# Loads in pieces, early products of the identity, and weight chunks rounded one place sooner, at the start of an attention and feed-forward kernel

## The chip, the cores and the metric

The kernel runs on one core of one Trainium2 chip. The metric is the device time of one execution in microseconds, which is the time of that core. Engines are named as in the profile: PE is TensorE (PEld its weight loads), DVE is VectorE, ACT is ScalarE, POOL is GpSimd, SP is the engine whose queue issues the loads. All runs used for a comparison of times are of the state "fast".

## The reference

The input x (4 batches of 12416 rows of 128) goes through two attentions with 32 inducing points, then through a gated feed-forward block.

```python
def mab(q, kv):
    s = scale * (q @ kv.transpose(0, 2, 1))
    s = s - s.max(-1, keepdims=True)
    a = np.exp(s); a /= a.sum(-1, keepdims=True) + 1e-09
    return a @ kv
h = mab(I, x)                    # 32 rows per batch
y = mab(x, h)                    # 12416 rows per batch
xn = y / sqrt(mean(y * y) + 1e-06) * rms_g
out = (silu(xn @ w_gate) * (xn @ w_val)) @ w_out      # 128 -> 1536 -> 128
```

The three weights arrive as 64-bit floats and have to be rounded to 32 bits in the kernel. They are cut into nine chunks (i, c): i is 0 for w_gate, 1 for w_val, 2 for w_out, c is the third of the 1536 columns.

## The kernel before

Batch 0 is the start. Its x comes in seven sets (five of 16 rows per partition, one of 15, one of 2). TensorE turns each set into columns and makes scores; then come a maximum, exponentials, sums for h, and a chain that leads to the first products of the feed-forward loop.

```python
def load_rows(b, s):
    ...
    for t0, t1 in (((0, R), (R, 2 * R), (2 * R, n)) if not s else ((0, n),)):   # R is 4
        nc.sync.dma_start(out=t[:, t0:t1, :], in_=d[:, t0:t1, :])

def warm(n):                      # products that nobody reads
    ps = ps_acc.tile([P, 512], F32, name="acc")
    for _ in range(n):
        nc.tensor.matmul(ps[:, 0:P], ident[:], ident[:], start=True, stop=True)
```

Rounding a chunk is a sequence of small steps. VectorE masks out the exponent (power) and the upper mantissa bits (upper), ScalarE or VectorE makes numbers of them (power_number, upper_number), VectorE adds sign and lower bits (sign, lower), GpSimd multiplies the two parts, and the buffer of the raw words is filled with the next chunk.

```python
def sign():   # DVE
    nc.vector.scalar_tensor_tensor(out=e[:], in0=st["high"], scalar=-(1 << 31), in1=e[:], ...)
def lower():  # DVE, then POOL
    nc.vector.scalar_tensor_tensor(out=f[:], in0=st["low"].bitcast(U32), scalar=2.0 ** -52, in1=f[:], ...)
    nc.gpsimd.tensor_tensor(out=st["dst"], in0=f[:], in1=e.bitcast(F32)[:], op=ALU.mult)
    put()     # stores the chunk, and fetches the next raw one
```

The start, and the places of the chunks in the loop (k counts slots; a slot is one gate product, one value product and what hangs on them):

```python
for s in range(NS):
    for k in range(R):
        f["turn_x"](s, k)
    if s: f["scores1"](s - 1)
    if s == 2: parts(0, 0, nc.vector)       # power, power_number, upper, upper_number
    if s == 3: join(0, 0)                   # sign, lower
...
for s in range(NS):
    ...
    f["turn_e"](s)                          # DVE transposes e
    if s == 5: parts(1, 0)
    ...
    f["sum_h"](s)                           # PE
f["divide"](); f["turn_h"]()
...                                         # one chunk at each of the next few places
for k, one in ((0, (1, 1)), (3, (2, 1)), (7, (0, 2)), (10, (1, 2)), (13, (2, 2))):
    for j, name in ((0, "power"), (1, "power_number"), (1, "upper"), (2, "upper_number"), (2, "sign"), (3, "lower")):
        add(k + j, weight[one][name])
for k, *one in ((2, 0, 1), (5, 1, 1), (12, 0, 2), (15, 1, 2)):
    add(k, f["stack_of"], *one)             # PE product with the rounded chunk
    add(k, f["stack_low"], *one)            # DVE
```

Further names in the views: `stack_of` (L475) multiplies h with a rounded chunk of w_gate or w_val, L607 is the product with w_out, L657 and L662 are the gate and the value product, and `fold` adds up the four row groups of h before h is transposed (L409).

## Time and profile before

| | before |
|---|---|
| median of 3 runs | 1690.92 us (1689.47 to 1691.07) |
| TensorE busy | 98% of the profiled 1688.5 us |
| last scores of the first softmax end | 27.4 us |
| first gate product of the loop | 55.4 us |

The main views are shown in the prediction below. First, TensorE's timeline around 84 us: start, duration, engine and line, output from inputs, shape, count, and in brackets how long the engine was idle before it and what ended that.

```profile
83.97 0.39 PE L657 MATMUL gv<-a,sg 128*128 128x512 f32 x1
84.21 1.02 PE L607 MATMUL acc<-u,wo 128*128 128x512 f32 x2
84.66 0.80 PE L662 MATMUL gv<-a,sv 128*128 128x512 f32 x1
85.30 0.39 PE L657 MATMUL gv<-a,sg 128*128 128x512 f32 x1
86.93 1.13 PE L607 MATMUL acc<-u,wo 128*128 128x512 f32 x2 [1.24 <-POOL wo L283]
```

The sums for h on TensorE and the transposes of e that feed them on VectorE, from the timeline of the first 40 us.

```profile
31.73 5.63 PE L388 MATMUL gv<-xn,u 128*32 128x128 f32 x190
...
32.03 2.49 DVE L376 STREAM_TRANSPOSE u<-sc 128x512 f32<-128x512 f32 x4 [0.42 <-ACT sc L368]
```

TensorE does the 190 products without a hole, and four transposes run back to back beside them.

### The profile page before, as it was taken

To read this page: it belongs to the slowest core of one execution; us is meant where nothing else is said; L and a number is where in the kernel's file an instruction comes from. 1 tells how busy PE (TensorE), PEld (TensorE's weight loads), DVE (VectorE), ACT (ScalarE), POOL (GpSimd) and SP (SyncE) were. 2 spreads that over 40 slices of the span, in tenths; PEclk is the share of its full clock that TensorE was granted. 3 is DMA by queue.
4 is the path that set the end of the run, shared out by engine and by line. 5 is a ranking of instruction groups with operands and counts; after the bars stand their busy time and mean duration, and the time that the engine had idled before them with its cause. 6 is when DMAs were issued, how large, how long until landed. Compare 5 with 4: busy or idle time off the path is not lost.

```text
span 1688.5 us, 23205 instructions
## 1 busy us (share of the span) xinstructions
PE 1660.7 (98%) x6756; PEld 1036.6 (61%) x6756; DVE 1166.2 (69%) x1941; ACT 1237.4 (73%) x2216; POOL 1159.4 (69%) x931
## 2 busy tenths in 40 slices
PE   9989999999999999999999999999999999999998
PEld 6546665655676565665566666565557666666666
DVE  4877775676667776667667777676767666666665
ACT  4547777766787777776778777777677888788786
POOL 0336775777587775776668777577657888888884
PEclk9999999999999999999999999999999999999999
DMA  6445523433444131524335314252211111111111
GB/s 233 106 64 90 86 57 83 101 85 59 68 81 68 37 82 30 124 60 102 60 64 83 58 33 82 51 131 65 50 30 38 30 39 32 38 32 38 31 36 26
DMA packets 389454, 112.38 MB, mean 67 GB/s; under 512 B 365104, under 2 KB 369744, under 8 KB 386896
## 3 DMA queue, kind: packets, MB, share of 16 engines
q1 hardware_dynamic: 389136, 110.89, 32.1%
q8 instruction: 54, 0.88, 0.2%
q14 instruction: 72, 0.59, 0.1%
q10 hardware_dynamic: 192, 0.02, 0.0%
HBM read 53.95 MB, written 27.00 MB: 48 GB/s over the span
## 4 chain that ended last, share of the span: by engine, by line
PE 90%; ACT 2%; issue 1%; POOL 1%; DVE 1%; DVEq 0%; POOLq 0%; ACTq 0%
PE acc L607 42%; PE gv L657 17%; PE gv L662 16%; PE u L625 5%; PE u L623 5%; PE mm L330 3%; PE mm L509 1%; PE mm L388 1%; DVE u L664 1%; ACT silu L659 1%; ACT L659 1%; PE mm L461 0%; ACT L448 0%; POOL xn L650 0%; ACT sc L448 0%
## 5 line engine op out<-in xcount | busy, mean ns | idle before, releaser
L664 DVE TENSOR_TENSOR u<-silu,gv 128x512 f32<-128x512 f32 (+2 forms) x1200 | 788.0, 664 | 470.8 <-PE gv L662 236.0
L659 ACT ACTIVATE silu<-gv 128x512 f32<-128x512 f32 (+2 forms) x1200 | 698.6, 584 | 376.4 <-PE gv L657 340.0
L607 PE MATMUL acc<-u,wo 128*128 128x512 f32 (+2 forms) x1600 | 794.1, 580 | 3.5 <-DVE u L664 2.2
L662 PE MATMUL gv<-a,sv 128*128 128x512 f32 (+2 forms) x1188 | 760.2, 640 | 0.9 <-DVE u L664 0.6
L645 POOL TENSOR_TENSOR xn<-u,xn 128x512 fp32r<-128x512 f32 (+2 forms) x400 | 503.4, 1258 | 366.8 <-ACT xn L644 329.3
L650 POOL TENSOR_TENSOR xn<-hs,u 128x512 fp32r<-128x512 f32 (+2 forms) x400 | 503.6, 1259 | 39.3 <-ACT hs L649 36.1
L657 PE MATMUL gv<-a,sg 128*128 128x512 f32 (+2 forms) x1188 | 486.2, 409 | 6.0 <-ACT silu L659 6.0
L657 PEld LDWEIGHTS gv<-a,sg 128*128 128x128 f32 x1188 | 224.9, 189 | 238.3 <-ACT silu L659 120.6
L607 PEld LDWEIGHTS acc<-u,wo 128*128 128x128 f32 x1600 | 298.6, 189 | 82.6 <-issue 16.4
L662 PEld LDWEIGHTS gv<-a,sv 128*128 128x128 f32 x1188 | 224.7, 189 | 194.5 <-issue 137.7
L644 ACT ACTIVATE xn<-u 128x512 fp32r<-128x512 f32 (+2 forms) x400 | 247.7, 619 | 25.6 <-DVE u L664 23.7
L649 ACT ACTIVATE hs<-xn 128x512 f32<-128x512 f32 (+2 forms) x400 | 245.8, 614 | 4.9 <-POOL xn L650 4.0
L607 PE MATMUL acc<-xn,xn 128*128 128x512 f32 (+2 forms) x400 | 156.5, 391 | 4.5 <-POOL xn L650 4.5
L625 PE MATMUL u<-xn,xn 128*128 128x512 f32 (+2 forms) x400 | 155.7, 389 | 0.0
L623 PE MATMUL u<-xn,xn 128*128 128x512 f32 (+2 forms) x400 | 155.3, 388 | 0.0
L607 PEld LDWEIGHTS acc<-xn,xn 128*128 128x128 f32 x400 | 75.0, 188 | 24.2 <-POOL xn L650 7.6
L524 POOL TENSOR_TENSOR rs<-ms,mhalf 128x16 f32<-128x16 f32 (+2 forms) x28 | 75.9, 2709 | 16.9 <-DVE ms L522 15.1
L625 PEld LDWEIGHTS u<-xn,xn 128*128 128x128 f32 x400 | 75.2, 188 | 18.1
L623 PEld LDWEIGHTS u<-xn,xn 128*128 128x128 f32 x400 | 75.1, 188 | 16.8 <-issue 0.7
L616 DVE STREAM_TRANSPOSE o<-o 128x512 f32<-128x512 f32 (+2 forms) x97 | 67.7, 698 | 3.4
L615 DVE TENSOR_TENSOR o<-acc,o 128x512 f32<-128x512 f32 (+2 forms) x97 | 64.9, 669 | 0.0
L628 ACT ACTIVATE o<-u 128x512 f32<-128x512 f32 (+2 forms) x97 | 56.4, 582 | 0.0
(165 smaller groups left out, 745.1 us busy)
## 6 DMA issues: line engine op xcount, KB each, us to landing
out_dram<-o SPq DMA_DIRECT2D x320, 64.0 KB, 1.9
xn<-in_x_dram SPq DMA_DIRECT2D x62, 256.0 KB, 4.8
xT<-in_x_dram SPq DMA_DIRECT2D x60, 256.0 KB, 5.4
a<-hi SPq DMA_DIRECT2D x156, 64.0 KB, 2.0
a<-lo SPq DMA_DIRECT2D x156, 64.0 KB, 2.0
w<-w SPq DMA_DIRECT2D x22, 256.0 KB, 3.1
xn<-in_x_dram SPq DMA_DIRECT2D x4, 1024.0 KB, 10.9
out_dram<-o SPq DMA_DIRECT2D x64, 60.0 KB, 1.9
```

Of the source, the lines that this page charges most:

```text
L524: nc.gpsimd.tensor_tensor(out=rs, in0=ms, in1=mhalf[rows, 0:n], op=ALU.pow)
L607: nc.tensor.matmul(acc[:, 0:T], lhsT, rhs, start=st["left"] == NJ, stop=st["left"] == 1)
L623: nc.tensor.matmul(ups[:, 0:T], w[:, i, :], hi, start=st["k"] == nk, stop=False)
L625: nc.tensor.matmul(ups[:, 0:T], w[:, NK + i, :], lo, start=False, stop=not st["k"])
L644: nc.scalar.activation(hi, v, AF.Copy, scale=1.0 - 2.0 ** -13)
L645: nc.gpsimd.tensor_tensor(out=lo, in0=v, in1=hi.bitcast(F32), op=ALU.subtract)
L649: nc.scalar.activation(hs[:, 0:T], hi.bitcast(F32), AF.Copy, scale=1.0 + 2.0 ** -12)
L650: nc.gpsimd.tensor_tensor(out=d, in0=hs[:, 0:T], in1=v, op=ALU.subtract)
L657: nc.tensor.matmul(g[:, 0:T], sg[:, ts(j, P)], a[:, 0:T], start=True, stop=True)
L659: nc.scalar.activation(sl[:, 0:T], g[:, 0:T], AF.Silu)
L662: nc.tensor.matmul(v[:, 0:T], sv[:, ts(j, P)], a[:, 0:T], start=True, stop=True)
L664: nc.vector.tensor_tensor(out=t[:, 0:T], in0=sl[:, 0:T], in1=v[:, 0:T], op=ALU.mult)
```

## The change

The intent is that TensorE reaches its full clock sooner and that x reaches it in smaller pieces, and that rounded weight chunks are ready before TensorE asks for them. Chunk (1,0) is rounded within the first softmax, and each later chunk takes the place of the one before it.

```diff
-            for t0, t1 in (((0, R), (R, 2 * R), (2 * R, n)) if not s else ((0, n),)):
+            for t0, t1 in (((0, R), (R, 2 * R), (2 * R, n)) if not s else ((0, 2 * R), (2 * R, n)) if s in (1, full - 1) else ((0, n),)):
@@
-    warm(4)
+    warm(6)
@@ the raw gate chunk is fetched one set later
-        for _ in range(1 if s == 1 else 4 if s == NS - 1 else 0):
+        for _ in range(1 if s == 2 else 4 if s == NS - 1 else 0):
@@
             f["turn_x"](s, k)
+            if not s and k < 2:
+                warm(1)
-        if s == 2:
+        if s == 3:
             parts(0, 0, nc.vector)
-        if s == 3:
+        if s == 4:
             join(0, 0)
@@ chunk (1, 0), all on VectorE, between the steps of the maximum and of e
+    one = weight[1, 0]
     f["max1"]()
+    one["power"]()
     f["max2"]()
+    one["upper"]()
     f["max3"]()
+    one["power_number"](nc.vector)
@@ in the loop over sets, after turn_e(s)
-        if s == 5:
-            parts(1, 0)
+        if not s:
+            one["upper_number"](nc.vector)
+        if s == 1:
+            one["sign"]()
+        if s == 2:
+            one["lower"]()
+        if s == NS - 1:
+            parts(2, 0)
@@ (cut: (2,0), (0,1), (1,1) take the places of (1,0), (2,0), (0,1); the clamp of the power moves from power to power_number)
-            for k, one in ((0, (1, 1)), (3, (2, 1)), (7, (0, 2)), (10, (1, 2)), (13, (2, 2))):
+            add(0, weight[1, 1]["sign"])
+            add(1, weight[1, 1]["lower"])
+            for k, one in ((1, (2, 1)), (5, (0, 2)), (8, (1, 2)), (11, (2, 2))):
@@
-            for k, *one in ((2, 0, 1), (5, 1, 1), (12, 0, 2), (15, 1, 2)):
+            for k, *one in ((2, 0, 1), (4, 1, 1), (11, 0, 2), (13, 1, 2)):
```

More of the change, by code (lines that the diff above doesn't have):

```diff
@@ L238, in numbers, with power @@
                 engine.tensor_scalar(out=to[:], in0=t[:], scalar1=mul, scalar2=add, op0=ALU.mult, op1=ALU.add)
-        def power(engine=nc.scalar):
+        def power():
             if i < 2:
@@ L255, in power @@
                                     op0=ALU.logical_shift_right, op1=ALU.bitwise_and)
-            if engine is not nc.scalar:
-                nc.vector.tensor_scalar(out=e[:], in0=e[:], scalar1=896.0, scalar2=1151.0, op0=ALU.max, op1=ALU.min)
         def power_number(engine=nc.scalar):
             if wide:
+                e = st["e"]
+                if engine is not nc.scalar:
+                    nc.vector.tensor_scalar(out=e[:], in0=e[:], scalar1=896.0, scalar2=1151.0, op0=ALU.max, op1=ALU.min)
                 numbers("e", -896.0 * (1 << 23), float(1 << 23), engine)
@@ L683, in parts @@
         one = weight[i, c]
-        one["power"](*engine)
+        one["power"]()
         one["power_number"](*engine)
@@ L696 @@
             f["turn_x"](s, k)
+            if not s and k < 2:
+                warm(1)
         if s:
             f["scores1"](s - 1)
-        if s == 2:
+        if s == 3:
             parts(0, 0, nc.vector)
-        if s == 3:
+        if s == 4:
             join(0, 0)
     f["scores1"](NS - 1)
+    one = weight[1, 0]
     f["max1"]()
+    one["power"]()
     warm(4)
     f["max2"]()
+    one["upper"]()
     warm(3)
     f["max3"]()
+    one["power_number"](nc.vector)
     warm(8)
@@ L723 @@
     f["square_h"]()
-    weight[1, 0]["sign"]()
+    weight[2, 0]["sign"]()
     f["stack_of"](0, 0)
@@ L728 @@
     f["sub_max"](0)
-    weight[1, 0]["lower"]()
+    weight[2, 0]["lower"]()
     f["exp2"](0, 1)
@@ L735 @@
     square()
-    parts(2, 0)
+    parts(0, 1)
     f["stack_of"](1, 0)
@@ L740 @@
     scale()
-    weight[2, 0]["sign"]()
+    weight[0, 1]["sign"]()
     for i in range(2):
         f["stack_low"](i, 0)
-    parts(0, 1)
+    parts(1, 1)
     apply()
@@ L747 @@
     split()
-    weight[2, 0]["lower"]()
     spread(0, 0)
@@ L752 @@
     gather(0, 2)
-    join(0, 1)
+    weight[0, 1]["lower"]()
     flowing.append(True)
```

## The prediction

Its sum came to -3.8 us. A low window, here and below, is a stretch at half clock of 3.41 us, as long as the two in this trace (from 54.83 and from 126.51 us).

> **What bounds the kernel now.** I read the page's chain first, then the stretches of the first 130 us, then the timeline and the waits of TensorE inside them. All of the change lies before the eighteenth slot of the feed-forward loop (a slot is one gate product, one value product and what hangs on them), so the question is what TensorE loses in the first 90 us.
>
> The page, its busy line and its chain that ended last:
>
> ```profile
> PE 1660.7 (98%) x6756; PEld 1036.6 (61%) x6756; DVE 1166.2 (69%) x1941; ACT 1237.4 (73%) x2216; POOL 1159.4 (69%) x931
> ...
> PE 90%; ACT 2%; issue 1%; POOL 1%; DVE 1%; DVEq 0%; POOLq 0%; ACTq 0%
> ```
>
> TensorE is busy 98% of 1688.5 us. Whatever is gained must come from its idle time or from time in which it runs slowly, and most of both lies at the start. The timeline of the first 18 us, TensorE's transposes of x (L321), shows the slow part:
>
> ```profile
> 4.37 1.11 PE L321 MATMUL gv<-ident,xn 128*128 128x128 f32 x4
> ...
> 5.75 3.22 PE L321 MATMUL gv<-ident,xn 128*128 128x128 f32 x12 [0.27 <-DMA xn<-in_x_dram]
> ...
> 9.59 3.65 PE L321 MATMUL gv<-ident,xn 128*128 128x128 f32 x16 [0.62 <-ACT xT L324]
> ...
> 14.49 1.97 PE L321 MATMUL gv<-ident,xn 128*128 128x128 f32 x16
> ...
> 17.38 1.97 PE L321 MATMUL gv<-ident,xn 128*128 128x128 f32 x16
> ```
>
> Columns: start, duration, engine and line, output from inputs, count. Sixteen transposes of one set take 3.65 us at 9.59 and 1.97 us from 14.49 on: until about 13.9 us TensorE runs at half speed. From 14.49 on sets start every 2.89 us (14.49, 17.38, 20.27, 23.17) with TensorE full, while x lands every 2.5 us: set 1 was issued at 2.13 and took 7.3 us, so it landed at 9.46; set 2 landed at 13.2, set 3 at 15.7, set 4 at 18.2. So x is ahead of TensorE from set 2 on, and the slow start is passed on whole to the end of this part, 27.4 us.
>
> The stretches (columns: busy us of each engine, then clock, DMA share, GB/s) and TensorE's waits between 56 and 100 us:
>
> ```profile
> 54.90:58.20 3.30, 3.29 (x11) 2.28 (x10) 3.27 (x4) 1.62 (x3) 2.67 (x2) 0.50 0.68 203
> 126.60:129.80 3.20, 3.20 (x6) 1.67 (x5) 1.85 (x3) 0.63 (x2) 0.00 (x0) 0.50 0.27 68
> ...
> 57.00:87.50 30.50, 27.63 (x78) 13.81 (x76) 26.51 (x43) 18.46 (x32) 8.07 (x7) 0.98 0.50 113
> ```
> ```profile
> PE acc L607 <- POOL wo L283: 1.2, 1, 1.2
> PE mm L475 <- POOL hs L283: 0.7, 1, 0.7
> PE mm L475 <- POOL w L283: 0.6, 2, 0.4
> PE gv L662 <- DVE sv L480: 0.3, 1, 0.3
> ```
>
> In the loop's first 30.5 us TensorE is idle 2.87 us, all of it for weights that are not rounded yet: L283 is the last step of rounding a chunk. VectorE is full there too (26.51 of 30.5). Twice the clock falls to 0.50 for 3.4 us, each time after a TensorE wait (1.69 us before L563 at 53.57; 2.7 us before L607 at 125.03).
>
> [...]a transpose every 0.213 us at first, then every 0.109; the low stretches last 3.41 us. [...]9.59 to 13.9 holds nearly nothing but transposes and ended in full speed. [...]the trace shows 431 to 439 GB/s between 9.6 and 16.4 us[...]. [...]here one masking step (L254) takes 0.42 us alone and 1.14 beside a GpSimd multiply.
>
> **The change, part by part.**
>
> *(a) Load and clock.* Set 1 comes as two halves (the first should land near 8.2 instead of all at 9.46), the gate chunk goes behind set 2, set 5 is cut too. warm(6) for warm(4) adds 4 products (each warm is two passes of 0.213 us), filling 3.2 to 4.05 while x is awaited; two single ones fill 5.3 to 5.75 and 6.65 to 7.05. So TensorE is busy from 1.35 to about 8 us without a hole over 0.1. The full clock began at 13.87 by the trace[...]: full clock by about 7 to 8.2. Set 1 is then done at 10.4 (bound by its second half), scores of set 0 take 1.0, set 2 has landed at about 12.0, set 3 at 15.7 as before, since the same bytes lie ahead of it. Set 3's transposes start at 15.78 and not at 17.38; after it TensorE binds as before. **-1.6 us**. DMA now sets this start, so a still faster clock gives no more.
>
> *(b) Chunk (1,0) moves into the softmax.* Six VectorE steps (0.42, 0.42, 0.43, 0.43, 0.69, 0.69 by the same steps of chunk (0,0) and (1,0)) go between the maximum and the transposes of e. The first four fit in holes: VectorE waited 0.45 before L345, 0.47 before L354, 0.88 and 0.42 before the transposes. Perhaps +0.1. The last two stand between the second, third and fourth transpose, which ran back to back (four in 2.49). TensorE takes 0.93 for each set of sums, transposes come every 0.62; with 0.62 more ahead of the third, then of the fourth, TensorE waits 0.3 twice: **+0.65**. In return (2,0)'s first steps move to where (1,0)'s were, all later chunks move up one place, and one chunk's 0.84 us of masking and one 0.69 leave the loop.
>
> *(c) Stage 38 to 55 us.* The same steps at the same places with another chunk. After the split only one 0.69 step is left before the first L664, where before there were three (the last one 1.77 long): the first u came at 57.07 although its silu was done at 56.83: **-0.2**.
>
> *(d) The loop's first slots.* Slots are about 1.33 us of TensorE. (1,1): its last step is at slot 1, its product at slot 4, before 3 and 5: the 0.7 goes. (0,2): 8 and 11 for 10 and 12: the 0.35 goes. (1,2): 11 and 13 for 13 and 15, the same distance, so its 0.26 stays, but the value product of slot 16 no longer waits for it: 0.31 goes. (2,2): last step at 14 and not 16: the 1.24 goes. Sum 2.6; as VectorE remains nearly full I take **-2.5**. The fetches behind them come earlier too, as each waits for the chunk before.
>
> *(e) Clock windows.* The two low windows cost an estimated 0.7 (around the loop's start, where latency hides part) and 1.7 us (half of 3.4). [...]Mean **-0.25**, but a swing of about 1.5.
>
> Sum: -1.6 + 0.1 + 0.65 - 0.2 - 2.5 - 0.25 = -3.8, so 1687.1 us.
>
> **Rivals.** *VectorE takes over in slots 0 to 14.* u, four and a half chunks of about 2.2 to 2.6 us and four stack steps come to some 22 us for 15 slots, 1.47 a slot against TensorE's 1.33. The trace's 26.51 of 30.5 speaks for it; against it, eight u buffers let VectorE lag, and the work is 1.5 less than before. It would leave half of (d): 1688.4. *The clock does not rise sooner*[...]: (a) still gets something, as set 1's first half fills the hole before 9.59, but only about 0.8: 1688. *The holes were already hidden* behind the 2.7 us wait at 125 or the exponentials at 107: [...]both move with the loop, so I doubt it; it would be 1690. *No cost in (b)*, if TensorE has slack at the sums: 1686.4.
>
> **Range and chances.** Nothing in the steady part changes, so 2% (34 us) is out of reach either way. The three runs before span 1.6 us; with (d) uncertain by 1.3 and (e) by 1.5, I take 1684.7 to 1689.4. Faster by over 2%: 0.005; within: 0.99; slower: 0.005.
>
> **What would show it.** (a) transposes of sets 1 to 3 at 1.97 us for sixteen, the last scores at about 25.8 and not 27.4. (b) two waits of TensorE of about 0.3 us for the transposes of e. (c) the first gate product at about 54.6. (d) TensorE's waits for L283 in the loop under 0.6 in sum. (e) where the clock is 0.50. Wrong if the early clock comes late, if the loop keeps 2 us of waits, or if a low window appears or goes: then only the clock view tells the parts apart.

## More of the kernel before

The product with wo (L607) normally starts 0.24 us after a gate product (83.97, 84.21). At 86.93 it starts 1.63 us after one, because chunk (2,2) was not rounded yet.

## The result, and the profile after

The changed kernel takes 1684.78 us (median of 4 runs, 1683.21 to 1685.48) against 1690.6 us for the kernel before (4 runs, 1689.47 to 1691.07). The ratio is 0.9965 with a 95% interval of 0.9948 to 0.9983. A ratio here is the mean time of one kernel's fast runs over that of the other's of the same rounds, so it is not quite the ratio of the medians. The mean of the four runs is 1684.56 us, 5.9 less than before. The prediction had 1687.1, 3.8 less, and a range of 1684.7 to 1689.4.

The page's busy line, the stretches and TensorE's waits between 55 and 100 us, in the changed kernel. The columns of the stretches are the busy times of PE, PEld, DVE, ACT and POOL, then clock, DMA share and GB/s.

```profile
PE 1657.2 (98%) x6764; PEld 1034.8 (61%) x6764; DVE 1165.0 (69%) x1944; ACT 1235.8 (73%) x2214; POOL 1159.1 (69%) x931
```
```profile
119.40:122.70 3.30, 3.30 (x6) 1.99 (x7) 2.59 (x5) 0.70 (x2) 1.28 (x1) 0.50 0.16 40
...
57.00:87.50 30.50, 30.50 (x100) 15.59 (x98) 27.30 (x50) 17.06 (x30) 7.46 (x6) 1.00 0.51 104
```
```profile
PE acc L608 <- DVE u L665: 0.3, 1, 0.3
```

In the loop's first 30.5 us TensorE was busy 27.63 us in 78 products and is now busy all 30.50 us in 100. Every wait for a weight is gone. VectorE is a little fuller than it was (27.30 us for 26.51). One stretch at half clock is left, at 119.4.

The start, on TensorE (lines are one higher than before, L322 for L321):

```profile
7.07 1.10 PE L322 MATMUL gv<-ident,xn 128*128 128x128 f32 x8
8.97 1.07 PE L322 MATMUL gv<-ident,xn 128*128 128x128 f32 x8 [0.81 <-ACT xT L325]
10.23 1.06 PE L322 MATMUL gv<-ident,xn 128*128 128x128 f32 x8 [0.19 <-ACT xT L325]
11.22 1.06 PE L331 MATMUL gv<-xT,indT 128*32 128x512 f32 x8
12.71 1.94 PE L322 MATMUL gv<-ident,xn 128*128 128x128 f32 x16 [0.42 <-DMA xn<-in_x_dram]
```

The transposes are at full speed from about 7 us on (one every 0.109 us, after one every 0.213), and TensorE now waits for x. The wait before 8.97 stands under ScalarE, but that set's first half landed at 8.84, as its load was issued at 2.13 and took 6.7 us. The sums for h, on the same engine:

```profile
30.79 6.28 PE L389 MATMUL gv<-xn,u 128*32 128x128 f32 x190
```

They take 6.28 us where they took 5.63. The record shows only two holes in them, of 0.11 and 0.12 us, at 33.05 and 34.25.

The start times of TensorE's landmarks show where the time came from. Gate products are counted from 0. From the last scores to gate product 38 a stretch repeats to 0.05 us in all runs that leave it alone, so there a single profile settles most questions. Three stretches do not repeat so well. The start hangs on when x lands: the last scores end at 26.22 to 27.57 us (mean 26.86) in the seven traces with the changed start, and at 27.44 and 27.89 in the two with the old one. Gate product 38 to 50 hangs on the clock (see below), and gate product 50 to the end differs by 0.3 us among kernels that are the same there.

| stretch | before | changed | difference |
|---|---|---|---|
| start to the end of the last scores | 27.44 | 26.50 | -0.94 |
| last scores to first sum for h | 4.29 | 4.29 | 0 |
| first sum for h to the transpose of h (L409) | 6.74 | 7.39 | +0.65 |
| transpose of h to the first product of the loop's input (L563) | 15.10 | 14.68 | -0.42 |
| that product to gate product 2 | 3.70 | 3.00 | -0.70 |
| gate product 2 to gate product 20 | 33.37 | 29.17 | -4.20 |
| gate product 20 to 50 | 50.03 | 49.94 | -0.09 |
| gate product 50 to the end | 1547.81 | 1548.07 | +0.26 |
| sum | 1688.48 | 1683.04 | -5.44 |

### The profile page after: what moved, and what is told of

Read it like the earlier page. It is cut to its first block, busy times and chain, and to the rows that moved or that the text cites. A ratio compares the mean times of both kernels' runs of the same rounds, so it can differ in the third digit from the quotient of the medians.

```text
span 1683.0 us, 23231 instructions
## 1 busy us (share of the span) xinstructions
PE 1657.2 (98%) x6764; PEld 1034.8 (61%) x6764; DVE 1165.0 (69%) x1944; ACT 1235.8 (73%) x2214; POOL 1159.1 (69%) x931
## 4 chain that ended last, share of the span: by engine, by line
PE 93%; ACT 2%; DVE 1%; issue 1%; DMA 1%; POOL 1%; SPq 0%; DVEq 0%; POOLq 0%; ACTq 0%
PE acc L608 43%; PE gv L658 17%; PE gv L663 16%; PE u L626 5%; PE u L624 5%; PE mm L331 3%; PE mm L510 1%; PE mm L389 1%; DMA xn<-in_x_dram 1%; ACT silu L660 1%; DVE u L665 1%; ACT L660 1%; POOL rs L525 0%; PE gv L322 0%; PE mm L462 0%
## 5 line engine op out<-in xcount | busy, mean ns | idle before, releaser
L608 PE MATMUL acc<-u,wo 128*128 128x512 f32 (+2 forms) x1600 | 793.5, 580 | 2.6 <-DVE u L665 2.5
L608 PEld LDWEIGHTS acc<-u,wo 128*128 128x128 f32 x1600 | 298.3, 189 | 81.1 <-issue 16.6
L608 PE MATMUL acc<-xn,xn 128*128 128x512 f32 (+2 forms) x400 | 156.7, 392 | 4.5 <-POOL xn L651 4.5
L608 PEld LDWEIGHTS acc<-xn,xn 128*128 128x128 f32 x400 | 75.1, 188 | 24.3 <-POOL xn L651 7.7
```

Of the source, the lines that this page charges most:

```text
L608: nc.tensor.matmul(acc[:, 0:T], lhsT, rhs, start=st["left"] == NJ, stop=st["left"] == 1)
```

## The experiments

The theory after the first look was this. The loop gained nearly twice what I had taken, because a wait costs TensorE more than the hole that the trace shows before it (4.20 us gained for 2.87 us of holes); the start gained less, because cutting a set makes x land later (set 3 at 16.33 for 15.71). The rivals were that the loop's gain belongs to the low clock window that was there before and is not there now, or to one chunk's work less on VectorE.

### The extra products alone

```diff
 (kernel before)
-    warm(4)
+    warm(6)
             f["turn_x"](s, k)
+            if not s and k < 2:
+                warm(1)
```

> The kernel before with the extra products of the identity alone (warm(6), and one product after each of set 0's first two groups); loads, chunks and loop as before. Theory E (the early full clock is what part 1 of the change gains): full clock by 7 to 8.2 us, set 3's transposes start near 15.8 us and not 17.38, the last scores end near 25.8 and not 27.44, and the time falls by about 1.6 us, more than the 0.94 that the whole change got there. Rival (the clock stays low because set 1 in one piece leaves a hole before 9.5 us): set 3 still at 17.4, time within 0.3 us of before. The loop's first slots (gate product 2 to gate product 20) stay at 33.4 us under both.

Measured: 1689.78 us (1689.66 to 1691.85), ratio to before 0.9999 (0.9984 to 1.0014). The trace has the full clock from 4.22 us, set 3 at 16.67 and the last scores at 26.73, 0.71 less than before. Set 3 landed at 16.15 and TensorE, full from 13.80 on, was behind it. Neither expectation holds: the clock came early even though there was a hole of 1.50 us before set 1 at 10.05, and the gain is less than half of 1.6. In the time it does not show beside the spread of the runs.

This run settled another point. It has no low window at the loop's start, and the stretch from L563 to gate product 2 takes 3.00 us like the changed kernel's, but gate product 2 to 20 takes 34.05 (33.4 was expected). Together that is 37.05, and 37.07 in the kernel before, which had the low window. TensorE's waits between 55 and 100 us in this run:

```profile
PE acc L607 <- POOL wo L283: 1.2, 1, 1.2
PE acc L607 <- DVE u L664: 0.8, 1, 0.8
PE mm L475 <- POOL hs L283: 0.7, 1, 0.7
PE mm L475 <- POOL w L283: 0.6, 2, 0.3
PE gv L662 <- DVE sv L480: 0.3, 1, 0.3
```

The 0.70 us that the low window cost at the loop's start was given back before gate product 20: without it, TensorE only waits longer, 0.8 us before an L607 that had no such wait in the kernel before. So the loop's gain from the chunks has to be read from L563 on, and is 37.05 - 32.17 = 4.9 us.

### The cut and the later gate chunk alone

The edits to load_rows, to the fetch of the gate chunk and to the places of chunk (0,0), on the kernel before.

> The kernel before with the two-piece loads of sets 1 and 5 and the gate chunk behind set 2 alone; no extra products. If the extra products are needed for the early clock: full clock at 13.9 us as before or one window (3.41 us) sooner at best, set 3 at 16.5 to 17.0, gain 0.4 to 0.9 us. If the cut itself makes the loads late (set 3 landed at 16.33 in the changed kernel, 15.71 before), set 3's landing shows 16.3 here too; if that was chance of one execution, 15.7.

Measured: 1689.94 us (1689.29 to 1691.54), ratio 0.9999 (0.9984 to 1.0014). The full clock began at 11.30, set 3 landed at 16.86 and started at 17.00, the last scores ended at 27.03, 0.41 less than before. So with the cut alone the full clock began 2.57 us sooner than in the kernel before (13.87), in one execution of each, and set 3 lands late here too.

### The changed kernel with sets 1 and 5 in one piece

```diff
-... else ((0, 2 * R), (2 * R, n)) if s in (1, full - 1) else ((0, n),)):
+... else ((0, n),)):
```

> The changed kernel with sets 1 and 5 loaded in one piece again (extra products, the gate chunk behind set 2, and chunks as changed). If the cut costs the 0.62 us by which set 3 landed later: set 3 lands at 15.7 and its transposes start near 15.8, last scores near 25.9 (changed kernel 26.50), time 0.6 us below the changed kernel. If the late landing was chance, or came from the order and not the cut: no difference over 0.2 us in the last scores. If the hole left by the one-piece set 1 holds the clock down: set 3 at 17 and 0.6 us or more above the changed kernel.

Measured: 1684.37 us (1682.67 to 1684.71), ratio to before 0.9962 (0.9946 to 0.9979), not to be told from the changed kernel. Set 3 landed at 16.06, but the last scores ended at 27.37: the third case that I had written, in the trace; the 0.6 us that it gave for the time did not show. Set 1 came at 9.94 after a hole of 1.49 us, and the clock, full from 6.83, fell back:

```profile
10.30:13.60 3.30, 3.30 (x19) 2.81 (x21) 0.00 (x0) 2.00 (x4) 0.00 (x0) 0.50 1.03 429
```

In the first run above nearly the same hole (1.50 us) was not followed by half clock. Why the one was and the other not is not shown. The first rise to full clock comes at 4.22 to 14.35 us in the fourteen traces.

### The chunks alone

The changed kernel with loads, gate chunk and products as before.

> The changed kernel with loads, gate chunk and products of the identity as before: only the places of the weight chunks are changed. Theory L (the waits for unrounded weights cost more than the idle time that the trace shows before them, 4.2 us for 2.87 us): gate product 2 to gate product 20 takes 29.2 us as in the changed kernel (33.4 before), whatever the start does; last scores at 27.4; the sums for h end 0.65 us later against their start than before; time 1686.3 to 1686.9 if the clock windows fall as before. Rival (part of the 4.2 us was the loop starting earlier against the loads, or the low clock window): 30.5 us or more for the same stretch.

Measured: 1684.91 us (1682.96 to 1687.63), ratio 0.9969 (0.9954 to 0.9984). Gate product 2 to 20 takes 29.15 us, the sums cost 0.65 more, the last scores ended at 27.89. **The chunks alone give nearly the whole change**: 5.4 us by the medians of this round, where the changed kernel had 5.8 by the medians of its own. The median is 1.4 us below the band that I expected. The four runs spread over 4.7 us, more than I expected, and the trace says why. The clock was at half for 6.83 us near 120, in the slowest of the four runs:

```profile
120.20:126.90 6.70, 6.11 (x10) 3.48 (x11) 3.93 (x7) 1.81 (x3) 1.82 (x2) 0.50 0.37 73
```

Gate product 38 to 50 measures it. It takes 17.5 us in the traces without a low window there, 18.9 to 19.2 with one window and 20.5 with two. Over the eleven traces that have the 2.7 us hole before it, none appeared three times, one six times, two twice.

### The old places in the loop

```diff
-for k, one in ((1, (2, 1)), (5, (0, 2)), (8, (1, 2)), (11, (2, 2))):
+for k, one in ((3, (2, 1)), (7, (0, 2)), (10, (1, 2)), (13, (2, 2))):
-for k, *one in ((2, 0, 1), (4, 1, 1), (11, 0, 2), (13, 1, 2)):
+for k, *one in ((2, 0, 1), (4, 1, 1), (12, 0, 2), (15, 1, 2)):
```

> The changed kernel with the four chunks that are still rounded inside the loop at the places of before ((2,1) at 3, (0,2) at 7, (1,2) at 10, (2,2) at 13, their products at 12 and 15); chunk (1,0) stays in the softmax and (1,1) early. Theory P (the places decide[...]): the holes before the second chunk's products and before the product that needs (2,2) come back, 0.3, 0.3, 0.3 and 1.2 us, and gate product 2 to gate product 20 takes 31.8 to 32.3 us (29.2 in the changed kernel, 33.4 before). Rival (one chunk fewer on VectorE inside the loop is what freed TensorE): 29.2 to 30.0 us, holes under 0.6 in sum.

The expected band allows about 0.2 us for each wait beyond its hole, an estimate from the 4.2 us gained for 2.87 us of holes.

Measured (one run, 1687.11 us, state unknown, so only the stretches are used): gate product 2 to 20 takes 32.40 us (0.1 over the expected band), 3.23 more than in the changed kernel. The waits came back:

```profile
PE acc L608 <- POOL wo L284: 1.2, 1, 1.2
PE mm L476 <- POOL w L284: 0.6, 2, 0.4
PE acc L608 <- DVE u L665: 0.3, 1, 0.3
PE gv L663 <- DVE sv L481: 0.3, 1, 0.3
```

VectorE had the same number of steps in the loop as in the changed kernel, so the rival "one chunk fewer on VectorE" falls: the places decide. The four holes that are new are 1.24, 0.35, 0.27 and 0.31 us, 2.17 in sum, and cost 3.23. That is 0.27 us for each wait on top of its hole.

### One wait by itself

```diff
-... (11, (2, 2))):
+... (13, (2, 2))):
```

> The changed kernel with chunk (2,2) alone rounded from slot 13 instead of 11, so that its last step is at slot 16 as before. If a wait costs the idle time that the trace shows: one hole h before the product with wo near slot 18, and gate product 17 to 20 grows by h over 5.17 us. If the idle time is read short, because the record of the product before reaches past the moment at which the next could have started: it grows by h + 0.2 to 0.3 us. h is between 0.6 and 1.3.

Measured (one run, 1687.50 us, state unknown): gate product 17 to 20 takes 6.67 us, 1.50 more than in the changed kernel (5.17), and this is the only stretch of the loop that grew. The hole is 1.23:

```profile
80.91 0.41 PE L658 MATMUL gv<-a,sg 128*128 128x512 f32 x1
81.15 1.02 PE L608 MATMUL acc<-u,wo 128*128 128x512 f32 x2
81.61 0.80 PE L663 MATMUL gv<-a,sv 128*128 128x512 f32 x1
82.24 0.40 PE L658 MATMUL gv<-a,sg 128*128 128x512 f32 x1
83.87 1.13 PE L608 MATMUL acc<-u,wo 128*128 128x512 f32 x2 [1.23 <-POOL wo L284]
84.43 0.80 PE L663 MATMUL gv<-a,sv 128*128 128x512 f32 x1
```

From gate product to L608 it is 0.24 us when nothing waits (80.91, 81.15) and 1.63 here, 1.39 lost. From L608 to the value product it is 0.46 (81.15, 81.61) and 0.56 here, another 0.10. The sum is 1.49. **The hole of 1.23 is what is left of 1.39 after the 0.16 us by which the record of the gate product reaches past the moment when the next product could have started.** The expectation was right on this.

### Chunk (1,0)'s last steps later

```diff
-        if s == 1:
+        if s == 3:
             one["sign"]()
-        if s == 2:
+        if s == 5:
             one["lower"]()
```

> The changed kernel with the last two VectorE steps of chunk (1,0) one after the fourth and one after the sixth transpose of e, where TensorE has slack. If those two steps cost the start 0.65 us: from the first sum for h to the product of fold takes 5.56 us as in the kernel before (6.21 in the changed one), no hole over 0.05 there, and 0.65 us less in all unless the clock windows move. Rival (something else, such as GpSimd's multiply, delays the transposes): still 6.1 or more.

Measured: 1685.53 us (1685.09 to 1686.51), ratio 0.9969 (0.9954 to 0.9984), no gain in time. The first sum to fold takes 5.57 as expected, so these two steps are what the sums waited for. But to the transpose of h it takes 7.07 (7.39 in the changed kernel): half was lost again. VectorE's timeline says where:

```profile
35.78 0.39 DVE L254 TENSOR_SCALAR we<-sc 128x512 int32<-128x512 int32 x1
36.09 1.50 DVE L267 TENSOR_SCALAR o<-sc 128x512 int32<-128x512 int32 x1
37.51 0.15 DVE L401 RECIPROCAL rl<-gv 128x1 f32<-128x1 f32 x1
```

Chunk (2,0)'s masking L267 took 1.50 us, where it takes 0.42 alone, beside GpSimd's multiply for (1,0), which the move had brought to the same moment. The reciprocal came late.

### That masking after the division

```diff
 (the edit above, and)
-            parts(2, 0)
+            weight[2, 0]["power"]()
+            weight[2, 0]["power_number"]()
     f["divide"]()
+    weight[2, 0]["upper"]()
+    weight[2, 0]["upper_number"]()
     f["turn_h"]()
```

> The changed kernel with the last two steps of chunk (1,0) after the fourth and sixth transpose of e, and chunk (2,0)'s second masking after the division. The run with the first of these moves ended the sums 0.64 us sooner and lost it again before the division, where VectorE was late. Theory (VectorE's work before the division is the bound of this stretch, not the places alone): first sum for h to the transpose of h takes 6.75 to 7.0 us (7.39 in the changed kernel, 7.07 with the first move, 6.74 before). Rival: 7.0 or more, the masking is missed later and the time comes back by the first gate product.

Measured: 1683.61 us (1682.59 to 1686.03), ratio 0.9961 (0.9947 to 0.9974). The first sum to the transpose of h takes 6.74 us, as in the kernel before, and nothing comes back later. The 0.65 us are avoidable. They came from the places of the two steps, and what was lost again in the run before came from the collision: VectorE stands idle for 0.93 us before the reciprocal here, which would have held the masking at its 0.42 us alone, but not at 1.50. No run separates this from my theory that the amount of VectorE's work is the bound, so for that part it is worked out and not shown.

```profile
36.98 0.17 DVE L401 RECIPROCAL rl<-gv 128x1 f32<-128x1 f32 x1 [0.93 <-PE gv L399]
```

### One piece, with the hole filled

The changed kernel with sets 1 and 5 in one piece, and warm(5) after set 0's last group.

> The changed kernel with sets 1 and 5 in one piece and five more products of the identity after set 0, which fill TensorE's hole of 1.5 us before set 1. If cutting set 1 costs landing time (set 3 landed 8.7 to 8.9 us after set 0's last piece in the four uncut runs, 8.9 to 9.5 in the six cut ones) and the hole costs the clock: full clock by about 7 to 8.5 us in every execution, set 3's transposes start at 16.1 to 16.3 (16.47 to 17.53 in the cut runs), the last scores end at 26.0 to 26.4. If not: 26.5 or later.

Measured: 1683.34 us (1682.94 to 1684.44), ratio 0.9958 (0.9944 to 0.9972). The full clock held from 6.16 us, set 3 landed at 16.18 and started at 16.32 (0.02 past the expected band), the last scores ended at 26.35. Set 3 landed at 15.71 to 16.18 in the six uncut traces (mean 16.06) and at 16.05 to 17.40 in the eight cut ones (mean 16.71). The cut costs about 0.65 us of landing on average, with a wide spread. The delay is there when the last piece of set 1 lands (9.80 to 11.16 us in the cut traces, 9.46 to 9.92 in the uncut ones); after it each MB takes 2.5 us in both. Why the two halves take longer than the whole I did not find out. In the time the uncut version with the filled hole is not to be told from the changed kernel.

### Without the split product before the second hole

The 2.7 us hole near 120 is in both kernels. GpSimd's power and a multiply stand before a step of a product that is split into three.

```diff
-            if (j not in KJ or b == 0 and u < 2 or ...
+            if (j not in KJ or b == 0 and u < 3 or ...
```

> The changed kernel, where the product of unit 2, j = 9 is no longer split into three on GpSimd, so that GpSimd's power (2.9 us) and its multiply do not stand before a step that TensorE waits for. Theory: the 2.7 us hole before L608 near 119.4 us goes, with it the low clock window of 3.41 or 6.83 us that follows it in most executions, while one plain product costs 0.2 us more than the split one; time 2.5 to 4.5 us below the changed kernel, spread of the runs smaller. Rival (the next split product takes over the same wait): a hole of 1 us or more before another L608 near 122, gain under 1.5.

Measured: 1683.61 us (1682.51 to 1684.67), ratio 0.9957 (0.994 to 0.9973). The gain of 2.5 or more did not come. A hole of 2.40 us is still there, now before another L608, and VectorE stands before it:

```profile
119.12 0.71 DVE L533 STREAM_TRANSPOSE aT<-sc 128x512 f32<-128x512 f32 x1 [2.30 <-POOL sc L529]
119.75 0.65 DVE L665 TENSOR_TENSOR u<-silu,gv 128x512 f32<-128x512 f32 x1
```

On VectorE the next u stands behind that transpose, which waited 2.3 us for the same GpSimd chain, so u was late. My rival had named the wrong successor, but it was right that the wait would move. The spread of the runs (2.2 us) did not shrink to that of the next section.

### And that transpose later

```diff
 (the edit above, and)
-(32, 33, 33, 34, 34, 36, 38)
+(32, 33, 33, 34, 34, 38, 40)     # the gathers that follow go two slots later too
```

> The run without the split product of unit 2, j = 9, and in addition the transposes of the second set's weights (L533) two slots later (38 for 36), with its split and its gathers two slots later too. That run still had a hole of 2.4 us, because VectorE itself stood 2.3 us before L533 for GpSimd's multiply. Theory: with both moved neither TensorE nor VectorE waits for that chain; gate product 20 to 38 as there, 38 to 50 takes 14.8 to 15.2 us (17.27 there, 19.13 in the changed kernel), no low clock window near 120 in any execution, time 1681.0 to 1682.0, spread under 1 us. Rival (the hole moves on to the gathers or to a split product): 38 to 50 stays over 16.5.

Measured: 1681.26 us (1681.24 to 1681.36), ratio 0.9945 (0.993 to 0.996). Gate product 38 to 50 takes 15.27 us (19.13 in the changed kernel; a little over the expected band). There was no low window, and the four runs lie within 0.12 us. The later transpose without the other edit was not run. TensorE's waits between 110 and 124 us:

```profile
PE acc L608 <- POOL xn L651: 0.7, 1, 0.7
PE u L626 <- POOL xn L646: 0.3, 1, 0.3
```

### All of these together

The edits of the last four sections and the uncut sets with the filled hole, together.

> The changed kernel with the three edits together (later seam and no split product of unit 2, j = 9; the softmax's rounding steps later; sets 1 and 5 uncut with five more products). If they are independent: 1680.0 to 1681.2 us, the changed kernel's 1684.8 less 3 to 4 for the seam and less 0.4 to 0.8 for the start. If the start's gain is taken back at the first gate product by GpSimd's power: 1681.2 to 1682.

Measured: 1680.59 us (5 runs, 1680.46 to 1680.97), ratio to before 0.9941 (0.9929 to 0.9954). It is the fastest version and gives the right result. Its stretches are those of the parts: last scores at 26.34, sums to transpose 6.74, gate product 38 to 50 15.28. The parts are independent.

## Why the prediction was right or wrong

*What bounds the kernel* was right: all that changed by more than 0.3 us lies before gate product 20, and TensorE's waits for unrounded weights were the largest part.

*Step (d), "Sum 2.6; as VectorE remains nearly full I take -2.5", failed in its size.* With (c)'s -0.2 it stood for 2.7 us from L563 to gate product 20; the chunks gave 4.9. The mechanism was the one named: the holes went. I took each wait for the hole in the trace. The runs with the old places and with (2,2) alone show that a wait costs its hole and 0.27 us more. The five holes of the run with the extra products alone are 0.71, 0.34, 0.27, 0.32 and 1.24, 2.88 in sum, and with five times 0.27 they are worth 4.2. Another 0.5 is the wait for the first u, which shrank from 0.84 to 0.31; in the kernel before it was hidden by the low window. These make 4.8 of 4.9. The rest I did not resolve. I had also counted 0.26 of (1,2) as staying; it went, although the distance of its two places was kept. And I had lowered the sum for a full VectorE. That rival fell: VectorE was busy 27.30 of 30.5 us, and TensorE waited for it only before the first u (0.31 us). Its sum was even too low: 15 steps and 4 steps of 0.69 us with 4.5 chunks of 2.2 to 2.6 make 23 to 25 us and not 22.

*Step (a), -1.6, was too large.* The early clock came, at 4.35 to 7.25 us in the seven traces with the changed start (about 7 to 8.2 was expected). The failing term is "Set 3's transposes start at 15.78", which took the landing of set 3 as fixed "since the same bytes lie ahead of it". It landed at 16.33, and at 16.71 on average over the cut runs. The profiled gain was 0.94, in one execution; by the seven traces with the changed start against the two with the old one it is 0.8. In the time neither the extra products nor the cut alone gave anything that shows (a ratio of 0.9999 for both).

*Step (b), +0.1 and +0.65, was right*: 0 and 0.65. Its mechanism was confirmed by moving the two steps. The sign that it named, two waits of about 0.3 us, came as two holes of 0.11 and 0.12: these too cost more than they show. It counts six VectorE steps where there are seven; the clamp of 0.42 us is missing, and it cost nothing here.

*Step (c)* had -0.2 for the first u. The transpose of h to L563 also shortened by 0.42: the product z on VectorE starts 1.23 us after the products with gram (L510) instead of 1.65. It does so in all eleven traces with the changed chunks and in none of the other three. The product behind those, which waits for GpSimd's rounded chunk, does not explain it: it starts 0.96 us after them in both kernels, and GpSimd's multiply ends 0.49 us after their start in both. The cause stays open.

*Step (e)* was wrong in one half. The low window at the loop's start costs nothing by gate product 20, as the loop waited for weights anyway, and it was in no trace but that of the kernel before. The other costs 1.3 to 1.7 us, or 2.9 when it lasts two windows, near the 1.7 estimated; it came in 8 of the 11 traces that have the 2.7 us hole before it. It appears in both kernels. That it is most of the spread of their runs is likely and not shown for each: the granted clock of an execution goes with its time (0.999 in the two faster runs of the chunks alone, 0.998 and 0.997 in the two slower).

The predicted 1687.1 was thus too high by 2.3 us against the median and 2.5 against the mean; 0.5 of the latter is the kernel before, taken as 1690.9 where the four runs have a mean of 1690.4. In the profiled pair the difference was 5.4 us for the predicted 3.8: (d) with (c) gained 2.2 more than predicted, the transpose of h to L563 another 0.4, and (b) cost 0.1 less; against that (a) gained 0.7 less, and (e) 0.4 less (a gain of 0.25 was expected, and 0.17 was lost after gate product 20).

## What to carry to other kernels

When an engine waits in a stream of instructions whose records overlap, measure the wait by the distance of starts, with it and without it, and not by the hole before the instruction; here holes of 0.3 us cost nearly twice that. Look for the wait that takes over when one is removed: two engines waited for the same GpSimd chain here, and moving one away left the other. And a hole in TensorE can cost more than itself through the clock. Here holes of 1.49 us (sets 1 and 5 in one piece) and 1.69 us (before L563 in the kernel before) were each followed by a stretch at half clock (0.50 over 3.3 us), and the hole of 2.7 us by 3.41 or 6.83 us of it in 8 of 11 traces, which cost 1.3 to 2.9 us; holes of 1.50 us (extra products alone) and 1.26 us (before L564 in the changed kernel) were not. So such holes come first.

## What else the traces showed

- In the run with the cut alone TensorE did nothing but transposes in the 3.41 us before the full clock (7.89 to 11.30), busy 3.26 of them. (The trace names them MATMUL; that they are transposes is taken from the call, `nc.tensor.transpose`.)

```profile
7.36 1.97 PE L321 MATMUL gv<-ident,xn 128*128 128x128 f32 x8 [0.31 <-DMA xn<-in_x_dram]
9.48 2.82 PE L321 MATMUL gv<-ident,xn 128*128 128x128 f32 x16 [0.15 <-DMA xn<-in_x_dram]
```

- A wait before the product with wo or a chunk's product (512 columns) cost 0.27 us more than the hole shown (3.23 us for 2.17 in four waits with the old places, 1.50 for 1.23 with (2,2) alone).
- With set 1 (1 MB) loaded in two halves, set 3 landed 0.65 us later on average (16.71 us in eight traces, against 16.06 in six).
- The profile's clock column reads 1.00 before its first clock record (0 to 13.9 us in the kernel before), while a transpose came every 0.213 us there and every 0.109 later. The distance of starts tells the clock there.
